# Decay-table arguments first, a second k^T bank, an idle bank for one mm1 unit, and one attention step moved: a fused linear-attention and MLP kernel on one core

## The chip, the cores and the metric

The kernel runs on one core of one Trainium2 chip. The metric is device microseconds of one execution; lower is better. The profile's span is from the first to the last instruction and lies 1.7 to 1.8 us under that time. The executions used here were in the fast state; four single looks have no state of their own (one execution each), but lie within the range of the fast runs. One outlier of the kernel before (324.79 us, labelled slow, granted clock 0.661) is left out of every mean. The granted clock is the share of TensorE's full clock that the profiler's record shows.

## The reference

Decayed linear attention over blocks of 64 positions, per batch and head, followed by an MLP with the activation h * tanh(softplus(h)) (Mish). Batch 4, 8 heads, 768 positions, head size 64; the MLP is 512 to 2048 to 512 on 3072 rows.

```python
for b in range(nb):                       # blocks of 64 positions
    intra = einsum('bhic,bhjc->bhij', qb, kb) * Dmask      # Dmask[i, j] = lam^(i-j) for i >= j
    intra = einsum('bhij,bhjd->bhid', intra, vb)
    inter = einsum('bhid,bhde->bhie', qb * lam_pow, kv_state)
    out[:, :, sl] = intra + inter
    kv_state = lam_block * kv_state + einsum('bhsd,bhse->bhde', kb * rev_pow, vb)
h = x @ w_in                              # x: the heads of out side by side
g = h * tanh(log1p(exp(h)))               # h above 20 taken as it is
return g @ w_out
```

## The kernel before

The kernel takes chunks of 128 positions, 6 groups (n) of 4 chunks, one for each batch (b). A half step (`hf`) is four heads of one chunk. Group 0's attention is the head of the program, with nothing beside it but filler matmuls (`busy`). Each later group's attention, att(n), is spread over the matmuls of the MLP (`mm1`, `mm2`) of the group before. A unit is one tile of mm1's output, four 128x512 matmuls.

Names in the lines of the profile: `pk` and `pq` are the PSUM tiles of the transposed k and q, `kz` and `qT` their copies in SBUF; `pS` the scores and `sb` the scores after the decay mask; `pO` the attention's output; `pv` the product of k and v for the state; `ph` and `hsg` mm1's output before and after Mish; `po` mm2's output.

Decay tables: `dm` is the decay mask of group 0, `lq`, `lk` and `lbc` the later scalings. Their logarithms times positions are formed on VectorE and exponentiated on ScalarE (ACT). `decays(0)` stands ahead of the loop, `decays(1)` and `decays(2)` inside it.

```python
    for i in range(B):
        nc.vector.memset(vz[i][:, :, D : 2 * D], 0.0)
    for i in range(2, B):
        nc.vector.memset(kn[i][:, :, D : 2 * D], 0.0)
    ...
    busy(3)
    lamb = ps.tile([128, H], F32, name="lamb", tag="pO")
    nc.tensor.matmul(lamb, one1, lam1, start=True, stop=True)
    busy(6)
    ...
    def decays(t):
        hh = H // 2
        if t < 2:
            for h in range(t * hh, (t + 1) * hh):
                nc.vector.scalar_tensor_tensor(out=dm[:, h, :], in0=rel, ...)
            nc.scalar.activation(dm[...half t...], dm[...half t...], AF.Exp)
        if t == 2:
            ...                                        # lnp, then the argument lq, on VectorE
            nc.scalar.activation(lk, lnb, AF.Exp, scale=ek)
            nc.scalar.activation(lq, lq, AF.Exp)
            nc.scalar.activation(lbc, lnp, AF.Exp, scale=float(C))
            nc.scalar.activation(lmt, lnb[:, 0:1], AF.Mish)   # brings the Mish table in
```

The three stages of a half step in group 0, and the loop that runs them:

```python
    def att_a(s):                                      # transposes of k and q by matmul
        ...
        pk = ps.tile([128, 2, 2, C], F32, name="pk", tag="pk")        # one bank
        ...                                            # 4 matmuls into pk, 2 into pq
        nc.vector.tensor_copy(s.qT, pq)
        nc.scalar.activation(s.kz, pk, AF.Copy)        # k^T out of PSUM, on ACT
    def att_s(s):                                      # scores into pS (one bank), times dm: sb, on VectorE
        ...
    def att_o(s):                                      # sb times v into pO, copied to xt on ACT
        ...
    def mm1_part(n, ni, lo, hi):
        if lo == 0:
            ph_t[ni] = ps.tile([128, GT], F32, name="ph", tag="ph", bufs=2)
        ...                                            # 4 matmuls, 128x512 when whole
    decays(0)
    for t in range(nh + 2):                            # nh = 8 half steps
        if t < nh:
            att_a(first_halves[t])
        if 0 <= t - 1 < nh:
            att_s(first_halves[t - 1])
        if 0 <= t - 2:
            att_o(first_halves[t - 2])
        if t < 2:
            decays(t + 1)
        if t < nh + 1:
            busy(2 if t < 4 else 1)
    for ni in range(2):
        mm1_part(0, ni, 0, GT - C)
```

## Time and profile before

| | before |
|---|---|
| median of 3, then of 4 runs | 226.57, then 226.45 us |
| the profiled execution | 225.85 us, span 224.1 |
| TensorE busy | 214.6 us |
| TensorE's longest wait | 2.1 us, in the head |

The prediction shows the lines. The busy table says which engine has least to spare; the wait list of TensorE says who ended each idle stretch of it; the chain in order of time shows what stood before that. A number to keep in mind: the execution that was profiled took 225.85 us, the median of the runs 226.57.

### The profile page before, as it was taken

The numbers are of one execution on the slowest core, as the hardware profiler recorded it, in microseconds if no ns is written. First come the engines' busy times: TensorE is split into PE (matmuls) and PEld (weight loads), VectorE is DVE, ScalarE is ACT, GpSimd is POOL, SyncE is SP. The second block draws the span as 40 slices with busy tenths as digits, with TensorE's granted clock in tenths as the row PEclk, the third lists the DMA queues.
The fourth block names the chain that finished last, engine by engine and source line by source line (L and its number), as shares of the span: only waits on it lengthen the run. The fifth ranks groups of instructions, "written<-read, shape, count | busy, mean of one in ns | idle before, by whom it ended". The sixth has DMA issues, their size and how long they took to land.

```text
span 224.1 us, 3806 instructions
## 1 busy us (share of the span) xinstructions
PE 214.6 (96%) x1468; PEld 118.4 (53%) x1468; DVE 108.3 (48%) x242; ACT 105.1 (47%) x202; POOL 109.5 (49%) x134
## 2 busy tenths in 40 slices
PE   7968999989999999999999999999999999999994
PEld 3846554457644555545555545555445555444442
DVE  7638941067614999109985309985235442000000
ACT  5377466156666522366522375512466423376120
POOL 8995336349995878807887408887000000000000
PEclk9999999999999999999999999999999999999999
DMA  7999999927899999962999932999951011200112
GB/s 145 153 171 207 207 206 159 138 97 50 121 167 114 140 114 165 146 141 27 117 144 134 166 76 48 99 146 133 157 126 23 3 47 47 94 3 0 47 47 95
DMA packets 101715, 24.75 MB, mean 110 GB/s; under 512 B 94914, under 2 KB 98754, under 8 KB 101698
## 3 DMA queue, kind: packets, MB, share of 16 engines
q0 software_dynamic: 77568, 13.24, 80.1%
q1 hardware_dynamic: 19632, 4.79, 12.9%
q10 hardware_dynamic: 4498, 6.49, 8.9%
q8 instruction: 11, 0.18, 0.3%
q14 instruction: 6, 0.05, 0.1%
HBM read 27.26 MB, written 6.29 MB: 150 GB/s over the span
## 4 chain that ended last, share of the span: by engine, by line
PE 91%; ACT 4%; DVE 2%; issue 1%; ACTq 0%; DVEq 0%
PE ph L403 37%; PE po L426 36%; PE pS L339 5%; PE pO L362 4%; PE busy L168 2%; PE pO L358 2%; PE pv L245 2%; PE pk L299 1%; DVE sb L343 1%; PE pq L308 1%; ACT osb L438 1%; ACT L203 1%; ACT hsg L417 1%; DVE dm L191 0%; ACTq L435 0%
## 5 line engine op out<-in xcount | busy, mean ns | idle before, releaser
L417 ACT ACTIVATE hsg<-ph 128x512 f16<-128x512 f32 x96 | 57.1, 597 | 32.5 <-PE ph L403 32.0
L426 PEld LDWEIGHTS <-hsg 128*128 128x128 f16 x400 | 36.2, 98 | 31.5
L343 DVE TENSOR_TENSOR sb<-pS,maskT 128x512 f16<-128x512 f32 x40 | 27.4, 685 | 20.3 <-PE pS L339 20.3
L438 ACT ACTIVATE osb<-po 128x512 f32<-128x512 f32 (+1 forms) x24 | 14.2, 592 | 44.9 <-PE po L426 44.4
L365 ACT ACTIVATE xt<-pO 128x256 f16<-128x256 f32 x48 | 17.9, 382 | 25.5 <-PE pO L362 23.6
L426 PE MATMUL po<-wout_84,hsg 128*128 128x512 f16 (+2 forms) x100 | 24.6, 370 | 0.0
L426 PE MATMUL po<-wout_86,hsg 128*128 128x512 f16 (+2 forms) x100 | 24.6, 370 | 0.0
L426 PE MATMUL po<-wout_87,hsg 128*128 128x512 f16 (+2 forms) x100 | 24.6, 370 | 0.0
L426 PE MATMUL po<-wout_85,hsg 128*128 128x512 f16 (+2 forms) x100 | 24.6, 370 | 0.0
L403 PE MATMUL ph<-xt,win_82 128*128 128x512 f16 x96 | 23.3, 379 | 0.0
L403 PE MATMUL ph<-xt,win_83 128*128 128x512 f16 x96 | 23.3, 379 | 0.0
L78 POOL DMA_DIRECT2D qn<-in_q_dram x23 | 20.7, 901 | 5.0 <-DMA wout_84<-in_moe_w_out_dram 1.7
L403 PE MATMUL ph<-xt,win_81 128*128 128x512 f16 x96 | 22.3, 379 | 0.0
L70 POOL DMA_DIRECT2D kn<-in_k_dram x20 | 18.9, 945 | 3.3 <-DMA wout_86<-in_moe_w_out_dram 1.7
L280 DVE TENSOR_TENSOR qT<-qraw,lq 128x256 f16<-128x256 f16 x32 | 16.8, 524 | 0.0
L221 POOL TENSOR_TENSOR ktil<-kn,lk 128x512 f16<-128x512 f16 x15 | 16.0, 1080 | 0.1
L433 DVE COPY osb<-po 128x128 f32<-128x128 f32 x1 | 0.3, 292 | 32.1 <-PE po L426 32.1
L403 PEld LDWEIGHTS <-win_81 128*128 128x128 f16 x96 | 9.2, 98 | 9.9
L403 PEld LDWEIGHTS <-win_82 128*128 128x128 f16 x96 | 8.8, 98 | 7.8
L403 PEld LDWEIGHTS <-win_83 128*128 128x128 f16 x96 | 8.8, 98 | 7.8
L284 DVE COPY kz_155<-kraw 64x256 f16<-64x256 f16 x16 | 4.7, 294 | 15.3 <-DMA kraw<-ktil 15.0
L245 PEld LDWEIGHTS <-ktil 128*128 128x128 f16 x80 | 7.5, 98 | 7.3
(210 smaller groups left out, 316.8 us busy)
## 6 DMA issues: line engine op xcount, KB each, us to landing
out_dram<-osb ACTq DMA_DIRECT2D x23, 256.0 KB, 2.4
qn<-in_q_dram POOLq DMA_DIRECT2D x23, 128.0 KB, 5.0
kn<-in_k_dram POOLq DMA_DIRECT2D x20, 128.0 KB, 4.6
win_81<-in_moe_w_in_dram POOLq DMA_DIRECT2D x1, 512.0 KB, 6.8
win_82<-in_moe_w_in_dram POOLq DMA_DIRECT2D x1, 512.0 KB, 9.6
win_83<-in_moe_w_in_dram POOLq DMA_DIRECT2D x1, 512.0 KB, 11.4
wout_84<-in_moe_w_out_dram POOLq DMA_DIRECT2D x1, 512.0 KB, 13.3
wout_85<-in_moe_w_out_dram POOLq DMA_DIRECT2D x1, 512.0 KB, 15.1
```

Of the source, the lines that this page charges most:

```text
L70: nc.gpsimd.dma_start(out=kn[i], in_=chunk_rows(k, i))
L78: nc.gpsimd.dma_start(out=qn[i], in_=chunk_rows(q, i))
L221: (nc.vector if i <= B or i >= (NG - 1) * B else nc.gpsimd).tensor_tensor(out=t, in0=kn[i][:, :, 0:D], in1=bc(lk, 2, D), op=ALU.mult)
L245: nc.tensor.matmul(pv[:, p, :].rearrange("p (a e) -> p a e", a=2), ktil[i][:, 4 * hf + 2 * p : 4 * hf + 2 * p + 2, :].rearrange("p h c -> ...
L280: nc.vector.tensor_tensor(out=s.qT, in0=qraw[i][:, 2 * hf : 2 * hf + 2, :], in1=lqh, op=ALU.mult)
L339: nc.tensor.matmul(psS[:, 2 * p + hp, :], s.kz[:, p, hp, :], s.qT[:, p, :], start=True, stop=True,)
L343: nc.vector.tensor_tensor(out=s.sb, in0=psS, op=ALU.mult, in1=bc(maskT, 1, 4) if s.n > 0 else dm[:, 4 * s.hf : 4 * s.hf + 4, :])
L365: nc.scalar.activation(dst, psO, AF.Copy)
L403: nc.tensor.matmul(ph_t[ni][:, lo:hi], win0[ni][:, kc, :] if ni < w else win[ni // w][:, kc, (ni % w) * 128 : (ni % w) * 128 + 128], xt[n] ...
L417: nc.scalar.activation(hsg[n][:, ni, :], ph_t.pop(ni), AF.Mish)
L426: nc.tensor.matmul(po[:, lo:hi], hsg[n][:, ki, b * C : (b + 1) * C], wout[part][:, kk, lo:hi], start=(ki == 0), stop=(ki == NKI - 1),)
L438: nc.scalar.activation(o, i, AF.Copy)
```

## The change

Its intent: get every decay argument off VectorE before the first copies of group 0 need VectorE, so that the exponentials and the load of the Mish table come early in ACT's order; let k^T alternate between two banks; start the head sooner with two fillers fewer; keep TensorE busy in the last wait of group 0; and let the third unit of mm1 not wait for the first unit's Mish.

```diff
-    for i in range(B):
-        nc.vector.memset(vz[i][:, :, D : 2 * D], 0.0)
-    for i in range(2, B):
-        nc.vector.memset(kn[i][:, :, D : 2 * D], 0.0)
...
-    busy(6)
+    busy(4)
...
-    def decays(t):
-        ...
+    for h in range(H):                       # all of dm, then lnp and lq, ahead of the loop
+        nc.vector.scalar_tensor_tensor(...)
+    for hf in range(2):
+        nc.scalar.activation(dm[:, hs, :], dm[:, hs, :], AF.Exp)
+    ...
+    nc.vector.tensor_tensor(out=lq, in0=bc(ei, 1, JP), in1=bc(lnp, 2, C), op=ALU.mult)
+    def head_rest(t):                        # called in the loop in place of decays(t + 1)
+        if t == 0:
+            ...                              # exponentials lk, lq, lbc
+        if t == 1:
+            nc.scalar.activation(lmt, lnb[:, 0:1], AF.Mish)
+        if t % 2 == 0 and t // 2 < B:
+            ...                              # the memsets of vz and kn, two or one at a time
...
-            pk = ps.tile([128, 2, 2, C], F32, name="pk", tag="pk")
+            pk = ps.tile([128, 2, 2, C], F32, name="pk", tag=("pk", "po")[s.seq % 2],
+                         bufs=1 + s.seq % 2)
...
-            ph_t[ni] = ps.tile([128, GT], F32, name="ph", tag="ph", bufs=2)
+            ph_t[ni] = ps.tile([128, GT], F32, name="ph", tag="po" if ni == 2 else "ph", bufs=2)
...
+        if t == nh + 1:
+            mm1_part(0, 0, 0, GT - C)
         if 0 <= t - 2:
             att_o(first_halves[t - 2])
...
-    for ni in range(2):
-        mm1_part(0, ni, 0, GT - C)
-    for i in range(B):
-        scale_k(i)
+    mm1_part(0, 1, 0, GT - C)
+    scale_k(0)                               # the others, and memsets, between the units of mm1(0)
...
-            for ni in range(2):
-                mm1_part(n, ni, 0, GT - C)
-                while late: ...
+            mm1_part(n, 0, 0, GT - C)
+            att_o(last)
+            mm1_part(n, 1, 0, GT - C)
```

The last hunk writes differently what the loop did before: the built program's order of matmuls is the same there.

## The prediction

> **What bounds the kernel now.** I read the page's busy table and chain first, to see which engine sets the end, then TensorE's own waits, then the chain in order of time for the stretches with waits, and last the timeline of TensorE alone where a start time was needed.
>
> The busy table and the chain that ended last, from the page of the kernel before:
>
> ```profile
> span 224.1 us, 3806 instructions
> ...
> PE 214.6 (96%) x1468; PEld 118.4 (53%) x1468; DVE 108.3 (48%) x242; ACT 105.1 (47%) x202; POOL 109.5 (49%) x134
> ...
> PE 91%; ACT 4%; DVE 2%; issue 1%; ACTq 0%; DVEq 0%
> ```
>
> TensorE is busy 96% of the span and is 91% of the chain; no other engine passes half. Only 224.1 - 214.6 = 9.5 us can be won by closing gaps. Some 3.2 us of that is the last output after TensorE's end (20.86 of 24.10 us busy in the window from 200 us on), and 1.2 us is the start. The change can work only on the rest, and on the filler matmuls (`busy`), which keep TensorE occupied but compute nothing.
>
> TensorE's waits, all of them (what waited, for what, us in total, times, longest):
>
> ```profile
> PE pk L299 <- ACT kz_157 L320: 2.1, 1, 2.1
> PE busy L168 <- DVE kzero L148: 1.2, 1, 1.2
> PE ph L403 <- ACT hsg L417: 0.9, 2, 0.5
> PE pk L305 <- ACT kz_155 L324: 0.9, 1, 0.9
> PE pO L362 <- DVE sb L343: 0.3, 1, 0.3
> PE pS L339 <- DVE sb L343: 0.3, 1, 0.3
> PE pk L299 <- ACT kz_156 L320: 0.2, 1, 0.2
> ```
>
> The first is in the head, the third occurs once after group 0's attention and once at group 1's start. Why ACT is late in the first, from the chain in order of time (start, us, what):
>
> ```profile
> 9.45 0.68 DVE sb L343
> 10.13 0.30 DVE lnp L198
> ...
> 10.71 0.70 DVE lq L199
> 11.41 0.02 issue
> 11.44 0.63 ACT lq L201
> 12.07 0.10 ACT lbc L202
> 12.16 0.02 issue
> 12.18 1.28 ACT L203
> 13.46 0.01 issue
> 13.47 0.20 ACT lmt L203
> 13.68 0.49 ACT kz_157 L320
> 14.17 0.04 issue
> 14.21 1.16 PE pk L299 x8
> ```
>
> The lq argument reaches VectorE only at 10.71, behind group 0's copies; the exponential and the load of the Mish table (1.28 us) follow in ACT's order, ahead of the copy of k^T that frees the only `pk` bank. TensorE stands still 11.9 to 14.2 us.
>
> **What the Trainium skill says.** ScalarE: Activation LUTs, What ACT_TABLE_LOAD costs, gives about 1283 ns for the load; the trace agrees (1.28). It adds some 1380 ns of drain, which the trace does not show: lbc ends at 12.16, the load starts at 12.18, lmt at 13.47. PSUM — Partial Sum Buffer, Specifications, gives 8 banks of 2 KiB; the kernel's tags (ph 2, po 2, pk, pq, pS, pO) take all eight, so a second k^T bank can only be borrowed from `po`, unused until pv and mm2. TensorE: Matmul & The Clock Gate, What's actually happening, says a cold array runs at half rate until a busy window of about 3.4 us has passed. The trace agrees in kind: the fillers of 512 columns start 0.43 us apart (3.94, 4.36, 4.79, 5.22), later matmuls of that size 0.22 apart.
>
> **The change part by part.** The order of instructions of the built program, compared with before, shows TensorE's is identical except for two fillers fewer and the last `pO` of group 0 now between the two parts of mm1(0). The waits that vanish are those of `pk` on ACT in group 0, and of the third mm1 unit on `hsg` in every group. The last step of att(1) already stood between the parts of mm1(1) in before: that part is bookkeeping, 0 us.
>
> *Fewer fillers.* Two cold ones at 0.43 bring the first pk from 5.64 to 4.8. k has landed (issued 0.74, 3.4 us to landing, 4.1), and q (1.31 + 4.2 = 5.5) is needed only after pk. But the array is then still cold: before it warmed at about 5.7. About four of the eight pk pieces run at 0.23 rather than 0.115 us, so pq begins near 6.2 against 6.61: 0.4 us won, not 0.86.
>
> *Arguments first.* DVE drops six memsets (4.53 - 2.69, about 1.6 us) from ahead of dm. lnb is out at 3.39, so eight dm operations (4 took 0.99 us) run 3.45 to 5.45; lnp 0.6, lq 0.7: done near 6.75, just as pq ends (6.65). ACT: exp table to 4.69, two dm exponentials to about 6.1, the first kz copy 6.3 to 6.9, lk, lq and lbc to 7.8, the second copy when pk ends (near 8.1) to 8.7, Mish load to 10.0, lmt to 10.2, third copy when its pk ends (near 10.1), to 10.75. So the table load falls between two copies and no matmul waits.
>
> *Second pk bank.* With it TensorE runs the head back to back. From the starts in before, a float32 half step costs pk 1.0, pq 0.11 (float16) to 0.46, pS 0.22, pO 0.22, two fillers 0.43. From pq at 6.2: filler 6.65, pk 7.1, pq 8.05, pS 8.5, fillers 8.7, pk 9.15 (before 9.93), pq 10.15, pS 10.3, pO 10.5, pk 11.15 (before 14.21), pq, pS, pO, fillers 12.7, pk(4) 13.1, pS(3) 13.45. Before, pS(3) started at 16.53: 3.1 us earlier.
>
> From there pace is not TensorE's: pS has one bank, and before its starts lie 1.165 us apart (17.70, 18.87, 20.03), which is 0.69 for sb, 0.38 for pS and two hops. A second pk bank changes nothing there. pS(7) comes at 13.45 + 4 x 1.165 = 18.1.
>
> *mm1(0) part inside the last wait.* pO(6), a filler and the 0.65 us part run 18.3 to 19.4, past the end of sb(7) near 19.25; pO(7) to 19.65, second part 20.3, two tails 0.44: 20.75. Before, the same point was 24.35.
>
> *Third unit on an idle bank.* Before it waited:
>
> ```profile
> 24.13 0.39 PE L403 MATMUL ph<-xt,win_78 128*128 128x128 f16 x4
> 24.98 1.02 PE L403 MATMUL ph<-xt,win_79 128*128 128x512 f16 x4 [0.46 <-ACT hsg L417]
> ```
>
> In this TensorE timeline the 0.46 is counted from the modelled end of the matmuls; the next could have followed at 24.13 + 0.22 = 24.35, so 0.63 goes. The third unit starts at 20.75 instead of 24.98: **4.2 us**. At group 1's start the same wait (63.18 against 62.55) gives **0.6 us**. Later groups show no such wait. Sum 4.8 us, and 226.57 - 4.8 = 221.8.
>
> Nothing is added to the path: moved memsets and the scalings of k go into VectorE's idle time between mm1 units.
>
> **The rivals.** *The weights or group 1's loads come too late.* They are paced by the DMA queue, not TensorE, and don't move up. For it: kn of chunk 4 lands at 17.7 + 18.8 = 36.5, and VectorE already waits for it. Against: att(1) would start near 40.6, when k, q and v of its first chunk have landed (36.5, 37.3, 38.2); win_81 lands at 19.35 against a need at 22.6, the last wout at 35.7 against 38.9. If some slack of 2 to 3 us proved false, the gain would fall to about 2 us, 224.5.
>
> *The single pS bank or VectorE becomes the bound earlier.* VectorE must now fit a copy, sb and one or two memsets of 0.27 into a step; every other step of the later half it has 0.28 + 0.69 + 0.27, about 1.1 of 1.165. If it slips by 0.2 in four steps, 222.6.
>
> *The Mish load still hits.* Its place is exact only if ACT's lq ends before pk(1) does, near 8.1. If VectorE is 0.7 us later than I have it, the load delays the third copy, but that is needed only at 12.2, so 1.4 us of slack absorbs it: I give this little weight.
>
> *The cold clock.* The warming time varies; a microsecond of added cold time costs about half of that. Before alone spans 225.79 to 226.58.
>
> **Range and chances.** 4.8 us is 2.1%, just past the limit of 2% (4.53 us), so the verdict is near even whatever the mechanism. The sums are read from the trace to some 0.3 us each, and the rivals lean towards less; a warmer start or one more closed gap would give more. I expect 221.8, eight in ten between 220.6 and 223.2. Faster by over 2%: 0.60; within 2%: 0.39; slower: 0.01.
>
> **What would show it.** The 2.1 us wait of pk gone from TensorE's list, and both waits of ph on hsg; the Mish load starting near 8.7 instead of 12.18; first pk near 4.8 but with its first pieces slow; pS starts still some 1.165 us apart in the second half of group 0; the third mm1 unit at 20.5 to 21.0; the 0.9 us wait of pk on kz_155 near 41 still there, since ACT's order around the outputs is unchanged; from then on everything about 4.2, after group 1's start 4.8 us earlier. The prediction is wrong if a DMA appears in TensorE's waits, if sb pacing sets in before step 3, or if a wait after group 1 takes the gain back.

## The result

The changed kernel took 220.19 us (median of 4 runs, 220.03 to 220.58) against 226.45 us (225.79 to 226.58): ratio 0.9731, 95% interval 0.9708 to 0.9755, so faster by 2.7%. A ratio here is the mean time of one kernel's fast runs over that of the other's of the same rounds, so not quite the ratio of the medians. The time lies under the stated range (220.6 to 223.2).

The busy table and the chain that ended last of the changed kernel:

```profile
span 218.8 us, 3803 instructions
...
PE 213.0 (97%) x1466; PEld 119.0 (54%) x1466; DVE 107.8 (49%) x242; ACT 105.3 (48%) x202; POOL 109.7 (50%) x134
...
PE 95%; ACT 2%; DVE 1%; ACTq 0%; issue 0%
```

All waits of TensorE of the changed kernel (what waited, for what, us, times, longest):

```profile
PE busy L163 <- DVE kzero L148: 1.2, 1, 1.2
PE pk L308 <- ACT kz_155 L327: 0.9, 1, 0.9
PE pS L342 <- DVE sb L346: 0.3, 1, 0.3
```

Of seven waits three are left. The idle 2.1 us ahead of k^T (and the 0.2 us on another k^T copy), both listed waits of ph on hsg and that of pO on sb are gone; the 0.9 us at the start of att(1) stays. ACT's timeline of the changed kernel shows the Mish load in its new place (start, us, what, and in brackets the idle time before and who ended it):

```profile
8.40 0.60 ACT L323 ACTIVATE kz_156<-pk 128x512 f16<-128x512 f32 x1 [0.37 <-PE pk L302]
9.02 1.28 ACT L200 ACT_TABLE_LOAD   x1
10.31 0.21 ACT L200 ACTIVATE lmt<-lnb 128x1 f16<-128x1 f32 x1
10.42 0.58 ACT L323 ACTIVATE kz_157<-pk 128x512 f16<-128x512 f32 x1
```

The load stands between two copies of k^T, at 9.02 instead of 12.18. The third unit of group 0, which the prediction shows at 24.98 after a wait, now follows without one (TensorE's timeline):

```profile
20.69 1.03 PE L406 MATMUL ph<-xt,win_79 128*128 128x512 f16 x4
```

Setting the starts of like instructions in the two profiled executions beside each other shows where the time was won:

| point | before, us | after, us | moved |
|---|---|---|---|
| scores of the 4th half step of group 0 | 16.53 | 13.40 | -3.13 |
| third mm1 unit, group 0 | 24.98 | 20.69 | -4.29 |
| Mish of the third mm1 unit, group 1 | 64.24 | 59.34 | -4.90 |
| second mm1 unit, group 2 | 95.30 | 90.60 | -4.70 |
| third mm1 unit, group 2 | 96.30 | 91.46 | -4.84 |
| ACT's last copy of the output (osb), group 5 | 220.00 | 214.78 | -5.22 |

The head gave 4.3 where 4.2 was foreseen (in part by luck, see below). Inside att(2) 0.2 us was lost: around 74 us the scores of one half step wait for VectorE's copy of k^T (that copy ends at 74.17, and the scores, begun at 73.99, take 0.58 us instead of 0.39). But from group 2 on each group start wins another 0.13 us. TensorE's timeline of the kernel before at such a start:

```profile
94.44 1.03 PE L403 MATMUL ph<-xt,win_77 128*128 128x512 f16 x4
95.30 1.03 PE L403 MATMUL ph<-xt,win_78 128*128 128x512 f16 x4
96.30 1.02 PE L403 MATMUL ph<-xt,win_79 128*128 128x512 f16 x4
```

The same point of the changed kernel:

```profile
89.73 1.03 PE L406 MATMUL ph<-xt,win_77 128*128 128x512 f16 x4
90.60 1.03 PE L406 MATMUL ph<-xt,win_78 128*128 128x512 f16 x4
91.46 1.03 PE L406 MATMUL ph<-xt,win_79 128*128 128x512 f16 x4
```

Starts 0.86 us apart are back to back. Before, the third unit came 1.00 us after the second: a wait of 0.13 us, which no list shows, because the unit ahead is drawn with a modelled end 0.17 us past the point where the next could have started.

The pair of profiled executions is 5.27 us apart in time (225.85 and 220.58), the medians 6.26. So two things had to be found out: what each part is worth, and what makes executions of one kernel differ.

### The profile page after: what moved, and what is told of

It is laid out like the page before. It is cut to its first block, busy times and chain, and to the rows that moved or that the text cites. A ratio compares the mean times of both kernels' runs of the same rounds, so it can differ in the third digit from the quotient of the medians.

```text
span 218.8 us, 3803 instructions
## 1 busy us (share of the span) xinstructions
PE 213.0 (97%) x1466; PEld 119.0 (54%) x1466; DVE 107.8 (49%) x242; ACT 105.3 (48%) x202; POOL 109.7 (50%) x134
## 3 DMA queue, kind: packets, MB, share of 16 engines
q1 hardware_dynamic: 19632, 4.79, 13.2%
HBM read 27.26 MB, written 6.29 MB: 153 GB/s over the span
## 4 chain that ended last, share of the span: by engine, by line
PE 95%; ACT 2%; DVE 1%; ACTq 0%; issue 0%
PE ph L406 38%; PE po L429 37%; PE pS L342 5%; PE pO L365 5%; PE busy L163 3%; PE pk L302 2%; PE pO L361 2%; PE pv L247 2%; PE pq L311 1%; ACT osb L441 1%; ACTq L438 0%; PE pk L308 0%; ACT xt L368 0%; ACT kz_155 L327 0%; DVE sb L346 0%
```

## Experiments

All runs gave correct results. Runs of one table row were timed against the kernel before in the same rounds.

| label | kernel | median us | ratio to before (95%) |
|---|---|---|---|
| base_again | before, again | 226.17 (22 runs) | 1.0001 (0.9987 to 1.0016) |
| third_only | before, third unit on the idle bank | 225.14 (17) | 0.9950 (0.9934 to 0.9965) |
| args_only | before, arguments first | 222.84 (6) | 0.9849 (0.9824 to 0.9874) |
| no_third | changed, third unit as before | 221.81 (4) | 0.9801 (0.9777 to 0.9825) |
| no_bank | changed, one k^T bank | 220.45 (4) | 0.9742 (0.9718 to 0.9767) |
| no_order | changed, both mm1 parts last | 220.48 (6) | 0.9757 (0.9733 to 0.9781) |
| after_busy6 | changed, six fillers | 221.23 (6) | 0.9781 (0.9758 to 0.9804) |
| after_busy2 | changed, two fillers | 221.42 (6) | 0.9781 (0.9751 to 0.9811) |
| after_again | changed, again | 220.35 (6) | 0.9747 (0.9720 to 0.9773) |
| after_again2 | changed, again | 220.44 (5) | 0.9745 (0.9714 to 0.9776) |
| after_lean | changed, no fillers in the first four steps | 219.69 (4) | 0.9714 (0.9690 to 0.9737) |
| after_lean_busy2 | the same, and two fillers at the start | 219.79 (5) | 0.9713 (0.9687 to 0.9739) |
| lean_memsets | after_lean, three memsets moved | 219.51 (5) | 0.9701 (0.9671 to 0.9731) |

**What scatters: when the array warms up.** My theories were A, that the sum was short by the hidden waits and the profile was of a short execution; B, that the moment at which TensorE's clock goes from half to full rate (the warming, counted from the span's start) differs between executions; and D, that the standstill in the head makes the array cold again (back to half rate) in some. "At a like warming" below compares two executions that warmed at nearly the same moment.

```diff
# base_again, base_look1, base_look2, base_look3: the kernel before, unchanged
# after_look1, after_again, after_again2: the changed kernel, unchanged
```

> The kernel before under another name, as a control and for a second profile. Theory A (my sum was only short by a hidden wait, and the profile I worked from was a short execution): ratio 1.000 to within 0.002, and a profile of a longer execution (226.4 or more) has the same steps as the first one, longer by 0.5 us or so in one place that can be named. Theory B (the rest is a later warming of the array in most executions of before): in a long execution the half-rate start lasts some 1 us longer than the 5.8 us of the first profile, and the start of the first k^T piece group is later or slower by 0.5 us.

> The kernel before, one more profiled execution. Its executions fall into groups near 225.85, 226.5 and 227.3. Theory B (when the array warms up decides which): the time of this one is 225.9 us plus 0.48 us for each us that the warming comes after 6.0 us, so a 226.5 warms near 7.3 and a 227.3 near 9. Rival D (the groups come from the 2.3 us standstill, after which the array is cold again in some executions, or from another wait): an execution of 226.5 or more with a warming at 6 us and a longer or new wait later.

> The same once more, for another execution of the kernel before: time 225.9 plus 0.48 per us of warming after 6.0 us under theory B; a wait or a slow stretch elsewhere under rival D.

> The same a third time: time 225.9 plus 0.48 per us of warming after 6.0 us under theory B; a wait or a slow stretch elsewhere under rival D.

> The changed kernel again, for more executions and a second profile. Theory B (what the two profiles, 5.27 us apart, leave open against 6.1 us of the medians is when the array warms up): its executions spread over some 2 us as those of before do (225.15 to 227.34), their mean is about 5.5 us below before, and a profile in which the array warms later than 6.3 us takes longer than 220.6. Theory C (the changed kernel has a shorter spread because it lacks the fillers): all within 220.0 to 220.6, mean 6.1 below before.

> The changed kernel, one more profiled execution. Two so far: warming at 6.35, 220.58; at 7.57, 220.98. Theory B: 220.3 plus 0.4 per us of warming after 6.0 us. Rival D has no standstill here, so no relation beyond the warming.

The trace keeps a record of the granted clock; its beginning is the warming. With the time that the first eight float32 k^T matmuls took in the chain:

| execution | warming, us | first pk x8, us | time, us |
|---|---|---|---|
| before, first profile | 5.79 | 0.92 | 225.85 |
| base_again | 5.98 | 1.01 | 225.86 |
| base_look2 | 6.11 | 1.08 | 225.80 |
| base_look1 | 6.67 | 1.34 | 226.37 |
| base_look3 | 7.38 | 1.68 | 226.53 |
| after_look1 | 6.21 | 1.53 | 220.31 |
| after_again2 | 6.29 | 1.57 | 220.36 |
| after, first profile | 6.35 | 1.60 | 220.58 |
| after_again | 7.57 | 1.71 | 220.98 |

The chain of base_look3, the kernel before in a late execution (start, us, what; the prediction's first profile had pk here for 0.92 us):

```profile
5.85 1.68 PE pk L299 x8
7.53 0.46 PE pq L308 x4
```

And of after_again, the changed kernel in a late one:

```profile
5.00 1.71 PE pk L302 x8
6.70 0.85 PE pq L311 x4
```

The same work takes up to twice as long until the warming and goes at full speed after it. Later on nothing differs: base_look3 has the same waits as the first profile, and its third unit of group 2 starts at 97.03 against 96.30. A microsecond of later warming costs 0.4 to 0.5 us in both kernels (0.68 over 1.59 us before, 0.67 over 1.36 after). In what was profiled of the kernel before, 225.80 to 226.53 us, B suffices and nothing speaks for D.

But none of its slowest executions was profiled, and the record speaks for D there. Of its 90 executions in the longer rounds 15 have a mean granted clock of 0.992, among them all ten from 227.11 us up; their mean is 227.00, that of the other 75 is 226.11. `third_only`, which keeps the standstill, has 3 such of 17 (0.991); the 62 executions of kernels without it have none (lowest 0.997). A loss of 0.8% of 225 us is 1.8 us of full clock, as much as 3.6 us at half rate would lose (an estimate). The fall of the clock after the work is not the reason: in the traces it comes 2.0 to 5.0 us after the last matmul, which ends some 3.2 us before the span does, so it can take 0.6 us, the 0.997. So a second cold stretch is likely in these, and it goes with the standstill; where it lies, no trace shows.

One more thing can be read from the records of the clock, in 18 of the 19 traces: the stretch at full rate lasts 211.63, 215.04 or 218.45 us, which is 62, 63 or 64 times 3.413 us. The clock, then, seems to change on a grid of that step. That the place of an execution's start on this grid sets its warming would fit, but was not tested.

At a like warming (6.11 and 6.21) the kernels are 5.5 us apart; at 7.38 and 7.57, 5.55. The means over the fast runs, 226.26 (90 runs of the kernel before, in the longer rounds) and 220.42 (all 16 of the changed one), are 5.8 apart; without the 15 at a clock of 0.992 it is 226.11, 5.7 apart.

**The arguments alone.** Order, fillers, banks and third unit as before. The moved memsets and scalings of k belong to this part: without the memsets out of the way VectorE could not form the arguments so early. The two were not tried apart.

```diff
# against the changed kernel
-    busy(4)
+    busy(6)
-    pk = ps.tile(..., tag=("pk", "po")[s.seq % 2], bufs=1 + s.seq % 2)
+    pk = ps.tile(..., tag="pk")
-    ... tag="po" if ni == 2 else "ph", bufs=2)
+    ... tag="ph", bufs=2)
# and both mm1_part(0, ni) after the loop
```

> The kernel before with the arguments first (and memsets and scalings moved) as its only change: one k^T bank, six fillers, third unit on its old bank, old order at the end of group 0. If ACT's order around the Mish load is all of the head's gain, as the run without the second bank says: the 2.1 us wait goes, the wait after it too, 3.0 us off the kernel before, 223.3. If the bank is needed after all once fillers and order are as before: 1 to 2 us off.

1.5% came, some 3.4 us in the means; at warmings of 6.12 and 6.11 us, 223.07 against 225.80, 2.7 us. TensorE's list has lost the 2.1 us wait of pk, with one bank:

```profile
PE busy L163 <- DVE kzero L148: 1.2, 1, 1.2
PE ph L405 <- ACT hsg L419: 0.9, 2, 0.5
PE pk L307 <- ACT kz L326: 0.9, 1, 0.9
PE pO L364 <- DVE sb L345: 0.3, 1, 0.3
PE pS L341 <- DVE sb L345: 0.3, 1, 0.3
```

This is about half of the whole (2.7 of 5.5 at a like warming, 3.4 of 5.8 in the means), and it needs no second bank.

**The second bank taken away.**

```diff
-            pk = ps.tile([128, 2, 2, C], F32, name="pk", tag=("pk", "po")[s.seq % 2],
-                         bufs=1 + s.seq % 2)
+            pk = ps.tile([128, 2, 2, C], F32, name="pk", tag="pk")
```

> The changed kernel with one k^T bank again; arguments still first. Each k^T group then waits for ACT's copy of the one before (0.6 us and hops), and the second and third copy bring the Mish load into the path again: TensorE would wait about 0.2 us before the second k^T group and about 1.5 us before the third or fourth. Expected 2 us slower than the changed kernel, 222.2. Rival (the order of the arguments alone did the work, the bank is idle luxury): at most 0.5 us, 220.7.

I expected 2 us, and there was nothing to see: 0.9742 against 0.9731 to 0.9747 for the changed kernel. The chain of the run without the bank shows why (start, us, what):

```profile
7.17 0.97 PE pk L301 x8
...
14.00 0.35 PE pk L301 x4
14.35 0.11 PE pq L310 x2
14.47 0.26 PE pS L341 x4
```

The copy of the first k^T runs from 6.33 to 6.93, under pq and the fillers, so the second k^T group waits for it by less than 0.1 us. In the later steps k^T does wait (0.35 us instead of 0.22), but pS would have waited for sb anyway: the 0.13 is given back two instructions later. The warming hides nothing: this execution warmed at 5.73 and took 220.14, the changed kernel at 6.21 took 220.31, and warming 0.48 us earlier is worth some 0.2 us by the slope above. The bank is a luxury here, with the step fillers in place; without them it was not tried.

**The third unit, alone and taken away.**

```diff
# third_only, on the kernel before; no_third is the reverse on the changed kernel
-            ph_t[ni] = ps.tile([128, GT], F32, name="ph", tag="ph", bufs=2)
+            ph_t[ni] = ps.tile([128, GT], F32, name="ph", tag="po" if ni == 2 else "ph", bufs=2)
```

> The kernel before with the third unit of mm1 on the idle bank as its only change. Theory A: 0.63 us at group 0, 0.63 at group 1, and 0.13 at each of the four later groups (the third unit starts 1.00 us after the second there, 0.86 elsewhere), 1.8 us in all, so 224.5 to 224.7 against 226.3 to 226.5. As predicted on record (no wait in later groups): 1.2 us, 225.2. Ratio 0.992 against 0.9945.

> The changed kernel with the third unit back on its old bank. Theory A: 1.8 us slower than the changed kernel, 222.0. As on record: 1.2, 221.4. If the head and the third unit interact (the wait in group 0 overlaps something else) less than either.

Taken away it costs 1.4 us in the means (221.85 of 4 runs against 220.42, from other rounds), which does not separate the two expectations of 1.2 and 1.8. Its trace does: the third units of groups 0 and 1 are late again by 0.63 us each, and those of groups 2 to 5 by the same 0.13 us, 1.8 in all. Its profiled execution (warm at 5.33, 222.01) is 1.9 us above that of no_bank (warm at 5.73, 220.14), which is as fast as the changed kernel; that is one pair. Added alone it wins 1.1 us in the means, and a new wait eats part of it. From TensorE's waits of third_only:

```profile
PE pv L245 <- DVE w L257: 0.4, 1, 0.4
```

With mm1 running earlier, pv catches up with VectorE, which has four scalings of k, four memsets and lbm to do first. The changed kernel spreads these between the units, and has no such wait. So a part that looked like tidying seems to make the third unit's gain whole in group 0; this is read from the two traces, and no run took the spreading alone away.

**The order at the end of group 0.**

```diff
-        if t == nh + 1:
-            mm1_part(0, 0, 0, GT - C)
...
-    mm1_part(0, 1, 0, GT - C)
+    for ni in range(2):
+        mm1_part(0, ni, 0, GT - C)
```

> The changed kernel with both parts of mm1(0) after the last pO again. The wait of pO for the last sb (0.34 us in the chain before, some 0.5 with the modelled ends taken off) comes back: 0.5 us slower than the changed kernel. Rival (the part of mm1 that fills it only shifts the wait to the tails): no slower.

The wait of pO on sb is back in the list (0.3). In the medians of the same rounds it is 0.13 us, within the noise; at like speed more: this execution warmed at 5.61 and took 220.54, when the changed kernel, which took 220.31 with a warming at 6.21, should have been near 220.0 (no_bank, as fast as it, took 220.14 at 5.73). Some 0.4 to 0.5 us, from one pair, not shown by the timing.

**The fillers.**

```diff
-    busy(4)
+    busy(6)                                  # after_busy6; busy(2) in after_busy2
```

> The changed kernel with six fillers again. If the cold array sets what two fillers are worth, as predicted on record: 0.4 us slower. If they are worth their whole 0.86 us: 0.9 slower. If the fillers help the array warm up earlier: no slower at all.

> The changed kernel with two fillers in place of four. Theory B (a filler only does work ahead of the same warming time): 0.43 us faster than four at a like warming time, less some 0.1 because k lands at 4.1 us and the fillers end at 3.95; the mean near 220.0 against 220.4. Rival E (what six fillers cost in the medians, 0.8 us, is a filler's full cold time): 0.8 faster, 219.6. Rival F (fewer fillers let the array warm later): warming later than 8 us in the profile and no gain.

Six cost 0.8 us in the means (221.21 against 220.43 in the same rounds). The profile of that run warmed at 6.57 and took 221.10, against 6.35 and 220.58: 0.52, of which some 0.1 is the later warming. So 0.4 at a like warming, as predicted, but from one pair; the means lie nearer to 0.9, and the runs don't decide. Two fillers were no gain at all: mean 221.20, and a warming after 8 us, which is what rival F said. From the chain of that execution:

```profile
4.22 2.04 PE pk L302 x8
6.26 0.85 PE pq L311 x4
```

pk starts 0.8 us earlier than with four, but all of it is cold: this execution warmed at 8.46 us, the latest of all. Whether fewer fillers cause later warmings or it was a draw, six runs (220.06 to 221.73) don't settle; the run after_lean_busy2, also with two, warmed at 6.25.

**Without the fillers of the first four steps.** Since TensorE no longer waits there, its fillers are on the path.

```diff
-        if t < nh + 1:
-            busy(2 if t < 4 else 1)
+        if 4 <= t < nh + 1:
+            busy(1)
```

> The changed kernel without the two fillers of each of the first four steps of group 0, where TensorE now has no wait. If TensorE is the bound there: up to 4 times 0.43 us off, stopped by the Mish load, which now frees the third k^T copy near 10.7 us while pS(2) would be due near 11.0: about 1.3 us off, 219.0. Rival F: the array warms later or cools again, and the time is no less than 220.4.

> Both: two fillers at the start and none in the first four steps. The Mish load then is the end of the head's chain: at most 0.2 us better than without the step fillers alone, 218.8. If the gains add: 218.6.

The execution of after_lean warmed at 7.58 us and took 219.76, against 220.98 of the changed kernel at 7.57: 1.2 us, as expected (1.3), in one pair; the means, from different rounds, are 0.7 apart (219.69 and 220.42). With two fillers at the start as well (after_lean_busy2) the mean is 219.67: the 0.2 to 0.4 us expected of it did not come. What stops after_lean is not the Mish load (its third k^T copy ends at 11.16), but VectorE. From the chain of after_lean:

```profile
10.58 0.69 DVE sb L346
...
11.27 0.27 DVE vz L203
...
11.55 0.27 DVE kn L205
11.82 0.27 DVE qT L321
12.08 0.63 DVE sb L346
```

Two memsets stand between sb and the next copy of q^T. The last version moves one of them to the idle time of VectorE in step 0, the other to step 4, and a third memset from step 4 to step 5.

```diff
-        if t % 2 == 0 and t // 2 < B:
-            ...
+        for z in {0: (vz[0], kn[2], vz[1]), 4: (kn[3],), 5: (vz[2],), 6: (vz[3],)}.get(t, ()):
+            nc.vector.memset(z[:, :, D : 2 * D], 0.0)
```

> The version without step fillers, with its memsets moved to where VectorE is idle: in its trace two memsets (0.54 us) stood in the chain between sb(1) and the copy of q^T(3). Theory: VectorE bounds the head there, so 0.5 us less than without the move, 219.2 against 219.7 at a like warming (7.6 us), and the pS wait before step 3 shorter. Rival: the chain then goes through the Mish load and the third and fourth k^T copy at once, no gain.

> The changed kernel on the same chip in the same rounds, so that the last two versions can be compared without the chip between them: 220.0 to 221.0, mean 220.4, 1.2 us above the version with moved memsets.

It took 219.62 in the mean, after_lean 219.69: no gain beyond noise. The trace of its profiled execution holds no record of the clock; its first k^T group, from 4.69 us, took 1.06 us in TensorE's timeline, as the second one of the changed kernel does at full rate (1.05), so it was warm by then. Its chain runs elsewhere:

```profile
3.42 2.19 DVE dm L182 x8
5.61 0.57 DVE lnp L190
...
6.47 0.69 DVE lq L191
7.16 0.34 DVE qT L318
```

With an early warming VectorE's arguments, which the change put ahead of the first copy, are what the head waits for. Both lean versions beat the changed kernel and the one before; against 220.56 of the changed kernel in the same rounds the last one is 0.9 us faster in the means.

## Why the prediction was wrong

1. **The bound** was right: TensorE, with the gains in the head's waits and at the group starts. What was to be seen in the profile came: the waits of pk and ph gone, the Mish load at 9.02 (8.7 foreseen), first pk at 4.79 and slow (1.60 us in the chain), scores 1.17 us apart in the second half of group 0, third unit at 20.69 (20.5 to 21.0), the wait on kz_155 still there, no DMA in the list.
2. **The step that failed is "Later groups show no such wait."** They did: 4 times 0.13 us, 0.5 us in all, visible in the table of starts, not in the list of waits. The prediction took the list of waits for the whole, although it had itself seen, at group 0, that such a wait is counted only from a modelled end; it names the wait "in every group" among those that vanish, and put a number on two of the six. By the starts, then, the third unit was worth 1.8 us (0.63, 0.63 and 4 times 0.13) instead of 1.2; in the means no_third puts it at 1.4.
3. **The starting value** was the other: 226.57 - 4.8. The terms were read in an execution of 225.85 us that warmed at 5.79; the median 226.57 is of executions that warm near 7.4, as base_look3 did (7.38, 226.53). The prediction took the warming as fixed near 5.7 us and gave its spread no number. The four runs of the changed kernel (220.19) happened to lie below its mean over 16 runs, 220.42. Gain at a like warming 5.5 us, forecast 4.8: 0.7 us of the miss of 1.6 is the size of the gain, the rest the state of the array in the runs on both sides. So the hidden waits alone would have left the time inside the range (221.8 - 0.5 = 221.3).
4. **The second bank** was given credit with the arguments for the 3.1 us of the head. The size was right, the credit wrong: no_bank is as fast. args_only alone won 2.7 us at a like warming.
5. **The times of the head** came close, in part by luck. The first pq began at 6.43 us, 0.23 later than forecast, because the array warmed at 6.35 and not near 5.7; the three float32 k^T groups after it took 0.89 us each and not 1.0, which gave it back, so that the scores of the fourth half step began at 13.40 (13.45 foreseen) and the third unit of group 0 at 20.69 (20.75). **Fillers** (0.4) fit one pair of executions, not the means (0.8); **the last step of att(1)** gave nothing, as said; the order's own worth is not resolved by the timing. Two sums of the prediction are wrong without consequence: 4.53 - 2.69 is 1.84, while the six memsets take 6 times 0.27, 1.6 us; and 0.28 + 0.69 + 0.27 is 1.24, more than the 1.165 it was to fit into. It fits because the three overlap: in the changed kernel a copy, sb and a memset take VectorE from 13.60 to the next copy at 14.70.
6. **Rivals**: loads did not come late. The single pS bank sets the pace of the second half, as written. VectorE had its arguments 0.4 us later than forecast (7.15 against 6.75) and the Mish load came 0.3 later, without a wait; it cost 0.2 us once, in att(2), not in the head. The cold clock was named as a rival, but not put into the range.

What stays open: what a filler is worth and whether the choice of fillers moves the warming; where the executions at a clock of 0.992 lose their time; and what is left of the 0.3 us between 5.5 (like warmings) and 5.8 (all runs) once those executions are out (5.7), which is inside the intervals of the ratios (0.972 to 0.977 for after_again).

## What to carry to other kernels

Find the wait, then ask what stood in order ahead of the engine that ended it: here a table load and the activations ahead of it, all behind a late argument, and moving the argument was worth more than another buffer. Read pipelined engines by the distance of starts between equal groups, group by group, because a wait shorter than the modelled end shows in no list. Before subtracting a gain read in one execution from a median, check that both are of the same state; and look at the granted clock of every execution, not only of those that were profiled.

## What the Trainium skill lacked or had wrong

- TensorE: Matmul & The Clock Gate, What you observe, gives the transition to full rate some 500 ns of run-to-run spread. In these runs the spread is wider: 5.79 to 7.38 us from the span's start in five executions of the kernel before, 6.21 to 7.57 in four of the changed one, and 5.33 (no_third) to 8.46 (after_busy2) over all kernels with a record, with the first matmul always at 1.19 us; it costs 0.4 to 0.5 us of a 220 us kernel for each microsecond. The remark of the same page, What's actually happening, that the moment depends on where in a free-running window of 3413 ns the first matmul lands fits this better than its 500 ns does: the full-rate stretches here are whole multiples of 3.413 us.
- ScalarE: Activation LUTs, What ACT_TABLE_LOAD costs, adds some 1380 ns of drain to the load. No run here shows it: the load takes 1.28 us, the activation ahead of it ends 0.02 us before it starts, and the next one starts 0.01 us after it (8.40 + 0.60, 9.02 + 1.28, then 10.31).
- Perfetto Trace Analysis, Tensor Engine Instruction (MATMUL, LD_WEIGHTS), says that the end of a matmul in the profile is an estimate, but no page says that a wait of TensorE can hide under it: four 128x512 matmuls are drawn 1.03 us long where the next four can start after 0.86, so a wait of up to 0.17 us has no idle time in the profile.
